# A backward pass on one core: sharing two PSUM copies between two engines, and reordering loads and small products in the weight-gradient tail

## The chip, the cores and the metric

The kernel runs on one core of one Trainium2 chip. The metric is the device time of one launch in microseconds (us), lower is better. The core has five engines that matter here, each with its own instruction queue which it works off in order: TensorE (PE in the profile; its weight loads are PEld), VectorE (DVE), ScalarE (ACT), GpSimd (POOL) and SyncE (SP). In this kernel POOL and SP mostly issue DMAs.

## The reference, cut to what matters

The reference is a training step of one transformer block: it returns the output and the gradients of all weights and of the input.

```python
h  = x + A(layernorm(x), mem0, Wq, Wk, Wv, Wo)      # attention over 64 segments of 32 tokens
h2 = h + (silu(n @ w_gate) * (n @ w_up)) @ w_down    # n = layernorm(h)

# A, for each segment s in turn:
hh = concat(mem, xs)                  # 8 memory rows + 32 tokens = 40 rows
q, k, v = hh @ Wq, hh @ Wk, hh @ Wv   # 16 heads of 256
p = softmax(mask(q k^T / 16)); o = (p v) @ Wo
mem = o[:8]                           # goes to the next segment
out = o[8:]

grads = vjp(h2)(grad_out)             # x, mem0, Wq, Wk, Wv, Wo, w_gate, w_up, w_down
```

The sizes are 2048 tokens, width 448, 16 heads of 256 (4096 columns in all), 1792 feed-forward columns, everything in bf16. The memory rows link the segments: forward they run from segment 0 to 63, backward from 63 to 0.

## The kernel before, in words

The kernel has four stages: the forward chain over the 64 segments, the feed-forward block with its backward, the backward chain over the 64 segments (`backward_chain`), and the weight gradients (`tail_phase`). A scheduler orders the instructions of each engine from priorities and data dependences; `tc.issue_after(x)` holds an instruction behind x. Once built, each engine's order is fixed.

**A backward segment.** TensorE first forms dO transposed (L1151, 128 matmuls), which is copied out of PSUM into `doT`. It then transposes dO to token-major form in two halves of eight transposes (`token_major(0)` and `(1)`, L1160); each half fills one PSUM tile `ph` of 128 x 1024 bf16 and is copied to `dO_sb` by the line that the change touches (L1161). L1169 forms dP in `pD`. VectorE turns it into dS in a chain of its own: L1176, the sum L1178, L1179 and L1181, which writes `dS_bd`. In VectorE's queue copies of head products (L75, the helper `evac`) stand between these; L76 is the same helper on ScalarE. The head products (L1128) come three times: for v they read `dO_sb` and P, for k they read Q and `dS_bd`, for q they read K and the turned dS, `dST_bd` (transposed at L1209). `rows_in` (L1200) multiplies the copied head products by the weights and sums them in `pH`. At the end L1218 and L1219 copy `pH`, L1222 sums four strips of it with `sel`, and L1226 writes the gradient of the memory rows into `do_roll`, from which the next segment's L1151 starts.

Four segments make a token tile t; r = s % 4 is the place in it, counted down. When r is 0 the tile is done, and 96 matmuls at L1264 with L1271 and L1279 behind them work on its memory rows and the layer norm. These have no place of their own: the scheduler spreads them over the next segments, L1264 over r = 3, 2 and 1, L1271 into r = 1.

**The tail.** Each group accumulates products over 16 or 20 row blocks in PSUM. `rows_by_d` (L1397) does so for Wo and w_down, `d_by_e` for the others. `d_by_e` handles width 448 as three full 128-row parts (L1375) and one 64-row part (L1380); `att` calls it for v, k, q in two halves of the heads each, passes hi = 0 to 5, each with q = 0 and q = 1; `up_grad` calls it for w_gate's and w_up's gradients, for two column parts each, after hi = 0 and hi = 2. The parameter `frees` says where the 64-row products go: if true after every four blocks, if false all at the end. It is false for the first half of each pair of calls.

In `att` the last four blocks are memory rows. They are fetched by POOL (L1340), packed by VectorE and ScalarE (L1345, L1347), transposed by TensorE in two steps through one PSUM buffer `ph` (L1354), and copied into the block's slot. `k.last_mm` is the matmul behind which these transposes are held. Two of the four fetches of a pass are issued ahead of it, two by the pass itself.

**The loads.** `_TailLoads` issues the tail's first loads on SP, in the last backward segment: `grads(0)` brings the gradient rows into `DCt` (L342 for four blocks of memory rows, then L346 and L347 in four strips), `outs` brings the stored attention outputs X_o into the slots of a ring (L356), `grads(1)` brings the last memory rows (L349). SP also issues the store of the mem0 gradient (L1232), the load of XN (L1236) and the last transpose (L1242), whose result POOL stores to DHb (L1244); L349 reads it back. The order of blocks is 16, 17, 18, 19, 15, 14, down to 0. POOL loads `grad_out` into `GO` after w_up's gradient (L1471); it is read by the last group, w_down.

Of the kernel before, what the change touches and what calls it, by code (L numbers as in the profile page):

```python
# [15 lines left out]
P = 128  # L16
# [297 lines left out]
class _TailLoads:  # L314
# [18 lines left out]
    def grads(self, part):  # L333
        k, D, S, NT, M, SEG = self.k, self.k.D, self.k.S, self.k.NT, self.k.M, self.k.SEG
        sync, DHb = k.nc.sync, k.dr["DHb"]
        dcx = DHb[0:S, 0:D].rearrange("(t r i) d -> r i t d", r=4, i=SEG)
        dcm = DHb[S:, 0:D].rearrange("(t r m) d -> r m t d", r=4, m=M)
        dc8 = DHb[0:S, 0:D].rearrange("(g s i) d -> g s i d", s=16, i=SEG)
        if part == 0:
            for g in range(k.NB - NT):  # L340
                with k.tc.issue_after(k.last_load.ins):
                    sync.dma_start(out=self.DCt[:, NT + g], in_=dc8[g, :, 0:M])  # L342
        for r in range(4):
            if part == 0:
                with k.tc.issue_after(k.last_load.ins):
                    sync.dma_start(out=self.DCt[32 * r:32 * r + 24, :NT], in_=dcx[r, M:SEG])  # L346
                    sync.dma_start(out=self.DCt[32 * r + 24:32 * r + 32, 4:NT], in_=dcm[r, :, 4:NT])  # L347
            else:
                sync.dma_start(out=self.DCt[32 * r + 24:32 * r + 32, 0:4], in_=dcm[r, :, 0:4])  # L349
# [682 lines left out]
def backward_chain(k: _K):  # L1032
    nc, tc = k.nc, k.tc
    S, D, M, H, Dh, HD = k.S, k.D, k.M, k.H, k.Dh, k.HD
    SEG, L, NSEG, NT, KC, DP, MC, DC = k.SEG, k.L, k.NSEG, k.NT, k.KC, k.DP, k.MC, k.DC
# [14 lines left out]
    dO_sb = A(52, 16, P)  # L1050
# [80 lines left out]
    for s in range(NSEG - 1, -1, -1):  # L1131
# [12 lines left out]
        with k.prio.crit():  # L1144
            pss = [k.ps1() for _ in range(4)]
            for j in range(MC):
                c = cj(j)
                b, jj = divmod(j, 8)
                for kc in range(KC):
                    with tc.issue_after(k.last_dh.ins) if s == NSEG - 1 and j == 0 and kc == 0 else nullcontext():  # L1150
                        nc.tensor.matmul(pss[b][:, jj * L:(jj + 1) * L], lhsT=WoT_sb[:, kc, c * P:(c + 1) * P],  # L1151
                                         rhs=do_roll[:, kc, sl, :], start=(kc == 0), stop=(kc == KC - 1))
# [3 lines left out]
            def token_major(hf):  # L1156
                ph = k.ps1()[:].bitcast(BF16)
                for i in range(8):
                    c0 = 2 * (8 * hf + i)
                    nc.tensor.transpose(ph[:, i * P:(i + 1) * P], doT[:, c0:c0 + 2, :].rearrange("p c n -> p (c n)"), ident[:, :])  # L1160
                nc.scalar.copy(out=dO_sb[:, 8 * hf:8 * hf + 8, :], in_=ph.rearrange("p (c n) -> p c n", n=P))  # L1161
            token_major(0)
            token_major(1)
            pD = k.ps1()
# [5 lines left out]
                                         start=(dc == 0), stop=(dc == DC - 1), skip_group_check=True)  # L1170
            if s == 0:
                k.tl.grads(0)
                k.tl.outs(0, 7, 0, 6)
            pD3 = pD[:, 0:8 * L].rearrange("p (h n) -> p h n", n=L)
            prod = k.f32("f2", 8 * L, "prod")[:].rearrange("p (h n) -> p h n", n=L)
            nc.vector.scalar_tensor_tensor(out=prod, in0=pD3, scalar=k.scale, in1=P_sb, op0=ALU.mult, op1=ALU.mult)  # L1176
# [112 lines left out]
def tail_phase(k: _K):  # L1289
# [72 lines left out]
    tl.outs(0, NB, 11, 16)  # L1362
    xo = tl.x

    def d_by_e(lhs_of, rhs_of, nblk, widths, store, at=None, frees=True):

        pa = accs(7)
        for b0 in range(0, nblk, 4):
            for fn in (at or {}).get(b0, ()):
                fn()  # L1370
            for b in range(b0, min(nblk, b0 + 4)):
                for kc in range(KC - 1):
                    for g in range(2):
                        w = widths[g]
                        k.last_mm = nc.tensor.matmul(pa[2 * kc + g][:, 0:w], lhsT=lhs_of(b)[:, kc * P:(kc + 1) * P], rhs=rhs_of(b, g),  # L1375
                                         start=(b == 0), stop=(b == nblk - 1), skip_group_check=True)
            for b in range(b0, min(nblk, b0 + 4)) if frees else range(nblk) if b0 + 4 >= nblk else ():
                for g in range(2):
                    w = widths[g]
                    k.last_mm = nc.tensor.matmul(pa[6][64 * g:64 * g + 64, 0:w], lhsT=lhs_of(b)[:, (KC - 1) * P:D], rhs=rhs_of(b, g),  # L1380
                                     start=(b == 0), stop=(b == nblk - 1), skip_group_check=True)
        for i in range(6):
            kc, g = divmod(i, 2)
            res = resbuf()
            evac(res[:, 0:widths[g]], pa[i][:, 0:widths[g]])
            store(kc, g, res[:, 0:widths[g]])
        res = resbuf()
        for g in range(2):
            evac(res[64 * g:64 * g + 64, 0:widths[g]], pa[6][64 * g:64 * g + 64, 0:widths[g]])
            store(KC - 1, g, res[64 * g:64 * g + 64, 0:widths[g]])  # L1390
# [29 lines left out]
    def att(hi, mem, after):  # L1420
        nm, oi, hf = halves[hi]
        o2 = OUT[oi].rearrange("d h e -> d (h e)")
        xt = load_x(nm, hf)
        for g in range(NG):
            xt[NT + g] = ring()
        for q in range(2):
            at = {}
            if q == 0:
                (f0, p0, t0), (f1, p1, t1), (f2, p2, t2), (f3, p3, t3) = mem
                at = {0: [p0, f2], 4: [lambda: t0(xt[NT]), p1, f3], 8: [lambda: t1(xt[NT + 1]), p2],  # L1430
                      12: [lambda: t2(xt[NT + 2]), p3], 16: [lambda: t3(xt[NT + 3])]}
            elif after is not None:
                at = {12: [after[0][0], after[1][0]]}

            def st(kc, g, r, q=q, hf=hf, o2=o2):
                e0 = (16 * g + 8 * hf + 4 * q) * P
                nc.gpsimd.dma_start(out=o2[kc * P:min(D, (kc + 1) * P), e0:e0 + 512], in_=r)  # L1437

            def rhs(b, g, q=q, xt=xt):
                return xt[b].rearrange("p (cl g n) -> p cl g n", g=2, n=P)[:, 4 * q:4 * q + 4, g, :]  # L1440
            d_by_e(lambda b: HC[:, b, :], rhs, NB, (512, 512), st, at, q == 1)

    def up_grad(nm, oi, after):
        xt = []
        for t in range(NT):
            x_t = ring()
            nc.sync.dma_start(out=x_t[:, 0:F], in_=dr[nm][t * P:(t + 1) * P, :])
            xt.append(x_t)
        for p0 in (0, 1024):
            ws = (512, min(512, F - p0 - 512))  # L1450

            def st(kc, g, r, p0=p0, oi=oi):
                f0 = p0 + 512 * g
                nc.gpsimd.dma_start(out=OUT[oi][kc * P:min(D, (kc + 1) * P), f0:f0 + r.shape[-1]], in_=r)

            def rhs(b, g, p0=p0, ws=ws, xt=xt):
                return xt[b][:, p0 + 512 * g:p0 + 512 * g + ws[g]]
            d_by_e(lambda b: HN[:, b, :], rhs, NT, ws, st, {8: [after[0][0], after[1][0]]} if p0 else None, p0 > 0)

    mems = [load_m(nm, hf) for (nm, _, hf) in halves] + [None]  # L1460
    mems[0][0][0]()
# [1 line left out]
    for hi in range(len(halves)):  # L1463
        att(hi, mems[hi], mems[hi + 1] if hi not in (0, 2) else None)
        if hi == 0:
            nc.gpsimd.dma_start(out=HN[:, 0:NT, :], in_=dr["HN"].rearrange("(t p) d -> p t d", p=P))
            up_grad("DGP", 7, mems[1])
        if hi == 2:
            up_grad("DU", 8, mems[3])
            GO = W(0, NB, D)  # L1470
            nc.gpsimd.dma_start(out=GO[:, 0:NT, :], in_=GO2.rearrange("(t p) d -> p t d", p=P))  # L1471

# [44 lines left out]
```

## Time and profile before

| | |
|---|---|
| median of 4 runs | 3098.64 us (3093.57 to 3112.2) |
| profiled execution: time, span of the core | 3099.75 us, 3097.9 us |
| TensorE busy, share of span | 2903.9 us, 94% |
| VectorE, ScalarE, GpSimd busy | 1333.8, 1114.0, 672.8 us |
| ScalarE copies at L1161 | 128 of 1015 ns mean, 123.3 us |
| backward chain, first and last L1151 | 1343.1 to 2387.3 us |
| first tail matmul | 2419.18 us |

The profile is one execution. In a timeline each row gives the start and the length in us, the engine, the line, what it writes and reads with its shape, and the number of instructions merged into the row; in brackets stands how long the engine had been idle and what ended that. Matmul ends are modelled, so the start of the next instruction says more than the end of a row. SP and POOL rows are the times of issuing a DMA, not of its landing.

### The profile page before, as it was taken

Reading aid. Unit: us, or ns where it says so; the run is one execution under the profiler, and the core shown is the slowest. Engines: PE = TensorE matmul, PEld = TensorE weight load, DVE = VectorE, ACT = ScalarE, POOL = GpSimd, SP = SyncE. Lnnn points to the kernel's source line nnn. Section 1 sums busy time; section 2 is a strip of 40 time slices with the busy share of each in tenths; the row PEclk is TensorE's granted clock in tenths of the full one; section 3 lists DMA queues with packets and bytes.
Section 4 is the critical chain, followed back from the end, with each engine's and each line's share of the span. In section 5 each row is a group of like instructions: output and inputs, shape, how many; then the busy total and the mean of one; then the engine's idle time right before and its main releaser. Section 6 shows DMA issues by size and latency. Waiting matters only on the chain.

```text
span 3097.9 us, 108337 instructions
## 1 busy us (share of the span) xinstructions
PE 2903.9 (94%) x47640; PEld 1738.6 (56%) x47650; DVE 1333.8 (43%) x3381; ACT 1114.0 (36%) x2634; POOL 672.8 (22%) x1507
## 2 busy tenths in 40 slices
PE   5999999999998999989999999999999899999999
PEld 3455555555554556666666666666666454444444
DVE  4555555555555577744444445444454001111110
ACT  2444444444444444434444344444443011111110
POOL 2222222222222222421221112212121111212111
PEclk9999999999999999999999999999999899999999
DMA  7566766766766999974554445545545998969961
GB/s 243 136 169 178 183 169 176 188 168 173 190 179 177 287 221 226 218 273 121 153 138 133 139 135 136 152 132 142 140 132 140 285 271 220 182 186 221 170 170 51
DMA packets 739468, 550.12 MB, mean 178 GB/s; under 512 B 600052, under 2 KB 635364, under 8 KB 736564
## 3 DMA queue, kind: packets, MB, share of 16 engines
q1 hardware_dynamic: 687956, 389.65, 52.3%
q0 software_dynamic: 51040, 153.54, 14.9%
q8 instruction: 374, 6.13, 0.8%
q14 instruction: 98, 0.80, 0.1%
HBM read 168.01 MB, written 234.23 MB: 130 GB/s over the span
## 4 chain that ended last, share of the span: by engine, by line
PE 65%; issue 15%; DMA 7%; DVE 6%; ACT 3%; POOL 2%; SPq 1%; POOLq 0%; ACTq 0%; DVEq 0%
PE po L1200 7%; PE psf L1151 7%; PE psf L535 6%; PE psf L652 5%; PE po L697 4%; PE psf L1128 4%; PE psf L890 4%; PE fx L1264 3%; PE fx L1014 2%; PE fx L464 2%; PE psf L1222 2%; DVE arA L75 2%; PE psf L549 2%; PE psf L1160 2%; PE psf L1397 2%
## 5 line engine op out<-in xcount | busy, mean ns | idle before, releaser
L75 DVE CAST arA<-psf 128x256 bf16<-128x256 f32 (+3 forms) x933 | 428.2, 480 | 784.6 <-PE psf L1375 233.7
L76 ACT CAST arA<-psf 128x96 bf16<-128x96 f32 (+5 forms) x915 | 353.1, 409 | 1015.4 <-PE psf L1375 254.7
L1200 PE MATMUL po<-arW,arA 128*32 128x448 bf16 x6144 | 346.2, 354 | 5.7 <-DMA arW<-Tq 3.3
L1375 PE MATMUL psf<-arW,arA 128*128 128x512 bf16 x980 | 249.9, 383 | 0.0
L1375 PEld LDWEIGHTS <-arA 128*128 128x128 bf16 x1440 | 137.0, 99 | 167.6 <-issue 18.6
L1151 PEld LDWEIGHTS <-arW 128*128 128x128 bf16 x8192 | 214.8, 96 | 25.1 <-issue 25.1
L1151 PE MATMUL psf<-arA,arW 128*128 128x40 bf16 x8192 | 218.2, 180 | 6.2 <-DVE arA L1226 5.1
L1200 PEld LDWEIGHTS <-arA 128*32 128x32 bf16 x6144 | 151.5, 96 | 116.2 <-ACT arA L76 9.5
L652 PE MATMUL psf<-arW,arA 128*64 128x512 bf16 x1536 | 216.5, 382 | 0.0
L535 PE MATMUL psf<-arW,arA 128*32 128x512 bf16 x3072 | 193.9, 385 | 12.6 <-DVE arA L738 12.6
L76 ACT CAST arB<-psf 128x64 bf16<-128x64 f32 (+3 forms) x384 | 121.9, 318 | 151.6 <-PE psf L539 106.7
L697 PE MATMUL po<-arW,arA 128*32 128x256 bf16 (+1 forms) x4096 | 141.2, 263 | 10.8 <-DVE arA L75 7.7
L890 PE MATMUL psf<-arW 128*128 128x256 bf16 (+1 forms) x1288 | 146.4, 274 | 3.0 <-DVE arA L75 1.7
L890 PEld LDWEIGHTS <-arW 128*128 128x128 bf16 (+1 forms) x1344 | 102.4, 97 | 53.3 <-issue 42.5
L1397 PE MATMUL psf<-arW 128*128 128x448 bf16 x525 | 113.0, 357 | 12.3 <-DMA arW<-X_o 12.3
L1161 ACT COPY arA<-psf 128x1024 bf16<-128x1024 bf16 x128 | 123.3, 1015 | 2.4 <-PE psf L1160 1.0
L1128 PEld LDWEIGHTS <-arW 128*128 128x128 bf16 x2048 | 86.4, 99 | 62.3 <-issue 58.1
L535 PEld LDWEIGHTS <-arA 128*32 128x32 bf16 x3072 | 70.4, 96 | 90.1 <-DVE arA L738 18.1
L76 ACT COPY arA<-psf 128x512 bf16<-128x512 bf16 (+3 forms) x142 | 84.3, 594 | 89.2 <-DVE arA L75 77.4
L464 PE MATMUL fx<-arA,arW 128*128 128x64 bf16 (+1 forms) x2048 | 84.6, 196 | 32.5 <-ACT arB L76 19.0
L697 PEld LDWEIGHTS <-arA 128*32 128x32 bf16 x4096 | 93.6, 96 | 32.9 <-DVE arA L75 11.1
L1437 POOL DMA_DIRECT2D out_dram<-arA x96 | 51.9, 547 | 275.0 <-DVE arA L75 274.6
(286 smaller groups left out, 4626.7 us busy)
## 6 DMA issues: line engine op xcount, KB each, us to landing
arW<-T SPq DMA_DIRECT2D x256, 128.0 KB
X_o<-arA SPq DMA_DIRECT2D x37, 512.0 KB
T<-arA SPq DMA_DIRECT2D x64, 256.0 KB
X_v<-arA POOLq DMA_DIRECT2D x32, 512.0 KB, 4.8
X_k<-arA POOLq DMA_DIRECT2D x32, 512.0 KB, 3.9
X_q<-arA POOLq DMA_DIRECT2D x32, 512.0 KB, 3.2
out_dram<-arA POOLq DMA_DIRECT2D x90, 128.0 KB, 5.1
VG<-arA SPq DMA_DIRECT2D x64, 160.0 KB
```

The source lines that it names most:

```text
L75: return nc.vector.tensor_copy(out=out, in_=in_)
L76: return nc.scalar.copy(out=out, in_=in_)
L464: nc.tensor.matmul(banks[w][:, i * 64:(i + 1) * 64], lhsT=lhsT, rhs=xr[lo:hi, kc, :], start=(kc == 0 and i == 0), stop=(kc == KC - 1), ski ...
L535: nc.tensor.matmul(banks[w][32 * q:32 * q + 32, :], lhsT=hT_roll[:, kc, sl, M:L], rhs=(Wq_sb, Wk_sb)[w][:, kc, col(q, b)], start=(kc == 0) ...
L652: nc.tensor.matmul(pV[b][64 * g:64 * g + 64, 0:512], lhsT=hT_flat[:, kc, sl * L:sl * L + 64], rhs=Wv_sb[:, kc, n * 512:(n + 1) * 512], sta ...
L697: nc.tensor.matmul(pO[32 * q:32 * q + 32, 0:w], lhsT=xblk[:, j, r * SEG:(r + 1) * SEG], rhs=Wo_sb[:, cj(j), 256 * dh:256 * dh + w], start= ...
L890: nc.tensor.matmul(ps[fp][:, f2 * 256:(f2 + 1) * 256], lhsT=Wt[lo:hi, kc, c * P:(c + 1) * P], rhs=xT[lo:hi, kc, :], start=(kc == 0 and f2 ...
L1128: nc.tensor.matmul(ps[b][:, i * 2 * L:(i + 1) * 2 * L], lhsT=lhs[:, at, :], rhs=rhs_bd[:, cl // 2, :, :].rearrange("p g n -> p (g n)"), st ...
L1151: nc.tensor.matmul(pss[b][:, jj * L:(jj + 1) * L], lhsT=WoT_sb[:, kc, c * P:(c + 1) * P], rhs=do_roll[:, kc, sl, :], start=(kc == 0), stop ...
L1200: nc.tensor.matmul(pH[32 * (j % 4):32 * (j % 4) + 32, 0:D], lhsT=blk[nm][:, j, r * SEG:(r + 1) * SEG], rhs=WT[:, cj(j), :], start=(nm == " ...
L1375: k.last_mm = nc.tensor.matmul(pa[2 * kc + g][:, 0:w], lhsT=lhs_of(b)[:, kc * P:(kc + 1) * P], rhs=rhs_of(b, g), start=(b == 0), stop=(b = ...
L1397: k.last_mm = nc.tensor.matmul(pa[i][:, 0:D], lhsT=lhs_of(b, i), rhs=rhs_of(b), start=(bi == 0), stop=(bi == m + 3))
```

## The change

It has four parts.

1. The two copies of a `token_major` pair are shared: the first half is copied by VectorE, the second by ScalarE. Before, ScalarE did both.
2. The loads of X_o blocks 16 to 19 (their first six column parts) are issued in `grads(0)`, between L342 and the strips of L346 and L347. Before, they came after the strips.
3. `frees` is gone: every call of `d_by_e` does its 64-row products after every four blocks. `k.last_mm` is set by these alone.
4. The load of `GO` is written after pass hi = 3 instead of after w_up's gradient. In the built program it stands behind the two M_k fetches of pass hi = 3 on POOL, where it stood ahead of them.

```diff
@@ grads(0)
                     sync.dma_start(out=self.DCt[:, NT + g], in_=dc8[g, :, 0:M])
+            self.outs(0, k.NB - NT, 0, 6)
@@ token_major
-                nc.scalar.copy(out=dO_sb[:, 8 * hf:8 * hf + 8, :], in_=ph.rearrange("p (c n) -> p c n", n=P))
+                k.evac(dO_sb[:, 8 * hf:8 * hf + 8, :], ph.rearrange("p (c n) -> p c n", n=P), "vs"[hf])
@@ last segment
-                k.tl.outs(0, 7, 0, 6)
+                k.tl.outs(4, 7, 0, 6)
@@ d_by_e
-    def d_by_e(lhs_of, rhs_of, nblk, widths, store, at=None, frees=True):
+    def d_by_e(lhs_of, rhs_of, nblk, widths, store, at=None):
...
-                        k.last_mm = nc.tensor.matmul(pa[2 * kc + g][:, 0:w], lhsT=lhs_of(b)[:, kc * P:(kc + 1) * P], rhs=rhs_of(b, g),
+                        nc.tensor.matmul(pa[2 * kc + g][:, 0:w], lhsT=lhs_of(b)[:, kc * P:(kc + 1) * P], rhs=rhs_of(b, g),
...
-            for b in range(b0, min(nblk, b0 + 4)) if frees else range(nblk) if b0 + 4 >= nblk else ():
+            for b in range(b0, min(nblk, b0 + 4)):
@@ att, up_grad
-            d_by_e(lambda b: HC[:, b, :], rhs, NB, (512, 512), st, at, q == 1)
+            d_by_e(lambda b: HC[:, b, :], rhs, NB, (512, 512), st, at)
...
-            d_by_e(lambda b: HN[:, b, :], rhs, NT, ws, st, {8: [after[0][0], after[1][0]]} if p0 else None, p0 > 0)
+            d_by_e(lambda b: HN[:, b, :], rhs, NT, ws, st, {8: [after[0][0], after[1][0]]} if p0 else None)
@@ the passes
             up_grad("DU", 8, mems[3])
+        if hi == 3:
             GO = W(0, NB, D)
             nc.gpsimd.dma_start(out=GO[:, 0:NT, :], in_=GO2.rearrange("(t p) d -> p t d", p=P))
```

## The prediction

> **What bounds the kernel now.** The page first: TensorE is busy 94% of the span, VectorE 43%, ScalarE 36%. So a copy on another engine costs nothing by itself; what counts is where TensorE stands still, and who ends the wait. Then, stage by stage, the timelines.
>
> *Backward stage* (1343 to 2407 us, 64 segments). TensorE in one segment, start and length in us:
>
> ```profile
> 2025.43 0.69 PE L1169 MATMUL psf<-arA 128*64 128x40 bf16 x32
> 2026.14 0.46 PE L1128 MATMUL psf<-arB,arA 128*128 128x80 bf16 x8
> 2026.53 0.56 PE L1264 MATMUL fx<-arW,arA 128*32 128x448 bf16 x8
> 2027.05 0.46 PE L1128 MATMUL psf<-arB,arA 128*128 128x80 bf16 x8
> 2027.44 1.70 PE L1200 MATMUL po<-arW,arA 128*32 128x448 bf16 x32
> 2028.97 0.36 PE L1264 MATMUL fx<-arW,arA 128*32 128x448 bf16 x4
> 2029.45 0.73 PE L1128 MATMUL psf<-arB,arW 128*128 128x80 bf16 x16
> ```
>
> ScalarE and VectorE in the same segment:
>
> ```profile
> 2025.07 1.93 ACT L1161 COPY arA<-psf 128x1024 bf16<-128x1024 bf16 x2
> ...
> 2026.16 0.49 DVE L1176 SCALAR_TENSOR_TENSOR prod<-psf,arB 128x320 f32<-128x320 f32 x1 [1.91 <-PE psf L1169]
> 2026.57 0.55 DVE L75 CAST arA<-psf 128x384 bf16<-128x384 f32 x1
> 2027.04 0.47 DVE L1178 TENSOR_REDUCE rsum<-prod 128x8 f32<-128x320 f32 x1
> 2027.55 0.42 DVE L75 CAST arA<-psf 128x256 bf16<-128x256 f32 x1
> ...
> 2028.48 0.83 DVE L1181 TENSOR_TENSOR arB<-prod,arB 128x640 bf16<-128x640 f32 x1
> ```
>
> The reader is to see two waits. The second eight v head products (2027.05) wait for the second L1161 copy (done 2027.00). But the k head products (2029.45) wait for L1181 (done 2029.31), the end of a VectorE chain that begins when L1169 ends (2026.12). That chain, 3.2 us, sets the segment; TensorE's work in front of the k heads is shorter. So what the copies delay is mostly given back at L1181.
>
> *Tail* (from 2407 us). TensorE and, last, the queues:
>
> ```profile
> 2419.18 2.05 PE L1397 MATMUL psf<-arW 128*128 128x448 bf16 x5 [12.04 <-DMA arW<-X_o]
> 2439.74 3.95 PE L1397 MATMUL psf<-arW 128*128 128x448 bf16 x20
> 2562.49 1.01 PE L1354 MATMUL ph<-ident,arB 128*128 128x128 bf16 x8 [6.33 <-DVE arW L75]
> 2859.93 1.01 PE L1354 MATMUL ph<-ident,arB 128*128 128x128 bf16 x8 [6.16 <-DVE arW L75]
> ...
> 2435.96 1.34 SPq L349 DMA_DIRECT2D arW<-DHb  x4
> 2844.43 1.19 POOL L1471 DMA_DIRECT2D arW<-in_grad_out_dram  x1
> 2845.61 0.78 POOL L1340 DMA_DIRECT2D arA<-M_k  x1
> 2858.84 0.43 DVE L1345 COPY arA<-arA 128x1024 bf16<-128x1024 bf16 x1 [11.37 <-DMA arA<-M_k]
> ```
>
> TensorE waits 12.04 us for the first X_o block. In pass hi=0 and hi=3 it waits 6.33 and 6.16 us at the transposes of a member block: the copy that frees `ph` stands on VectorE behind a pack (L1345) that waits for M_v or M_k. The same place costs 1.49 us in hi=1 (2676.49), 1.40 in hi=2 (2743.65) and 0.56 in hi=4 (2934.56).
>
> **What the Trainium skill says.** "TensorEngine Tiling (Array Packing)", Key Properties: a change of tiling mode drains TensorE. The trace agrees (0.23 us for a return trip, below). "TensorE: Matmul & The Clock Gate", What's actually happening: an idle window of about 3.4 us halves the clock until a busy window has passed. It agrees: after each wait of over 6 us, 512-column matmuls come 0.43 us apart instead of 0.215 for some 4.2 us. "VectorE: DVE Perf Modes", The perf-mode tier table: a copy out of PSUM has at most the double rate, fp32 none. It agrees: VectorE's copies of 1024 bf16 columns (the `ph` rows of L75) take 690 ns, those of 512 fp32 columns 687. "DMA: Bandwidth & Descriptors", Issuing engines are not separate DMA queues: all share 16 engines. It fits the 1.8 MB load of L1471 ahead of M_k: 13.2 us to the pack, against 8.6 and 9.7 in hi=1 and hi=2, where no such load stands in front.
>
> **The change part by part.** The built order of the changed program shows what moves.
>
> 1. *Copies.* 64 of 128 L1161 copies go from ScalarE (1015 ns) to VectorE (690, the row above), in front of L1176. The copy could start at 2025.07, when its transposes are done, and end at 2025.76, 0.40 before L1176 is due: nothing delayed. ScalarE's copy starts at about 2025.5 and ends at 2026.55, so the v heads end some 0.4 us earlier. The eight L1264 matmuls are then queued behind them: the same work, reordered. In the 49 segments outside the next item the k heads still wait for L1181. The only gain is inside the chain: the 256-column cast at 2027.55 starts 0.04 after TensorE's second eight ended (2027.51), while such casts otherwise start 0.08 before the end of the operation ahead (2027.51). So 0.12 us; I take 0.11: 49 x 0.11 = **-5.4 us**. Bounds 0 (another start cost) to -8.
>
> 2. *The r = 1 segments* (15). TensorE's order changes most: six L1271 matmul passes and the eight-product gap leave the way of the k heads, and VectorE now does the 256-column cast before L1181. Before: L1169 ends at 2042.16, k heads start at 2045.97, 3.81 later. After: the chain, cast included, 3.2; saves 0.6. Then eight L1271 passes at 0.115 (0.69 for six at 2045.28) and four L1200 stand before L1209, while eight L1200 leave: +0.5. At the end, L1271 and the 0.33 us wait for L1275 are gone: -0.3. Sum -0.4 each, 15 x 0.4 = **-6 us**; bounds +2 and -11.
>
> 3. *Start of the tail.* Four X_o loads are issued ahead of the eight slow DCt loads on SP (which took 2392.35 to 2407.4). So X_o blocks 16 to 19 are there when TensorE arrives. But the fifth block keeps its place behind the same bytes, and the last four blocks of the group need the rows of L349, issued 2435.96 to 2437.3, after SP waited for the DHb store. TensorE came to them at 2439.74. The 12 us wait moves there; I take **-1 us**, bounds +2 (a cold clock after the new wait) and -4.
>
> 4. *The 64-row products (L1380)* of eight passes (six first halves of att, two of up_grad) go from one block at the end into every group of four blocks. A block is 1.29 us. With 40 L1380 together, 2580.66 to 2586.49 less one block is 4.54 us; an interleaved eight, 2596.65 to 2599.03 less one block, is 1.09. Five of these are 5.45: 0.91 for four more trips, 0.23 each. Extra trips 6 x 4 + 2 x 3 = 30: **+6.8 us**. Results leave PSUM as in the second halves today, where the next pass follows without a wait (2617.84).
>
> 5. *What 4 gives back.* At the second member block two eights have been done, 2.2 us later in TensorE's order, while the M fetch lands when it did. Waits: hi=0 6.33 to 4.1; hi=1, hi=2, hi=4 (1.49, 1.40, 0.56) gone: -2.2 - 3.4 = **-5.6 us**. The clock of hi=0 still goes cold (4.1 is over 3.4); if not, another -2.
>
> 6. *The grad_out load* is now behind both M_k fetches on POOL. M_k is issued at 2844.4 and should land by 2854; TensorE needs the copy at 2856. The 6.16 us go, and with them the half-speed stretch (2562.49 to 2566.71 is 4.2 us for work of 2.1): -6.2 - 2.1 = **-8.3 us**. Behind grad_out stand the M_q fetches for hi=4, needed 55 us later; grad_out itself is read from 3050. Bounds -2.2 (M_k late anyway, only item 4's delay helps) and -8.3.
>
> Sum: -5.4 - 6 - 1 + 6.8 - 5.6 - 8.3 = -19.5. Against the profiled execution's 3099.75 us (span 3097.9) that is 3080.2; the median, 3098.64, lies 1.1 lower: **3079 us**.
>
> **Rivals.**
> *M_k is late for another reason* (the X_q transposes that start at 2826 fill the same engines). Then item 6 gives 2.2: -13.4, 3085 us. For it: DMA is 0.90 busy there. Against: 8.6 us in hi=1 at a share of 1.11.
> *The early loads pay in full.* If L349's rows come earlier, the whole 12 us can go: 11 more, 3068 us. Against: SP's order puts the OUT2 store, the transpose and the DHb store, for which L349 waits, behind the same bytes.
> *VectorE's copy is slow, and the time is longer.* Place: the queue ahead of L1176. No row of before has both engines copying 1024 columns out of PSUM at once with TensorE writing; if VectorE's copy then takes d, the chain starts d - 1.09 later in 64 segments. It decides from d = 1.40 us (64 x 0.31 = 20). At 1.5 us: +26 - 14 (items 2 to 6) = +12, 3111 us. Against: 690 ns in the `ph` rows, at most the 1015 of ScalarE.
>
> **How the numbers follow.** A measurement here tells about 0.5%, 15.5 us, from no change. Forecast 57%, M_k late 25%, full pay 12%, slow copy 6%. The range 3064 to 3098 takes in the first three with their bounds. Below 3083: three quarters of the forecast, the full pay and a fifth of M_k late: 0.60. Slower by over 15.5: most of the last, nearly 0.05. The rest 0.35.
>
> **What would show it.** Right: L1161's line gone from ScalarE for half its count, 64 VectorE copies near 0.69 us; r = 1 segments about 0.4 shorter than 16.9, others 0.1 shorter than 16.04; no wait at L1354 in hi=3, 4 us in hi=0; a wait of several us inside the first L1397 group, whose last four blocks start at about 2439 less the backward gain. Wrong: these segments unchanged, L1354 waiting over 5 us in hi=3, or L1176 starting later after L1169.

## The result

| | before | changed kernel |
|---|---|---|
| median, us (range, runs) | 3100.37 (3084.99 to 3131.32, 64) | 3084.82 (3069.95 to 3111.58, 43) |
| ratio, with 95% interval | 1 | 0.9955 [0.9943, 0.9967] |
| profiled execution: time, span, us | 3099.75, 3097.9 | 3090.31, 3088.5 |

The change saves 13.9 us by the ratio, with an interval of 10.2 to 17.7 (0.0045, 0.0033 and 0.0057 of 3100). Forecast was 19.5. The profiled execution lies 5.5 us above the median of its own kernel, so it shows less of the gain than a typical one.

### The profile after

Lines of the changed file from L343 on are one higher than before (L1160 is now L1161, L1176 is L1177, L1354 is L1355); the copies of L1161 now run at the helper lines L75 and L76.

The groups by shape show that half of the copies moved. The columns are line, engine, operation, tiles, count, then busy us and mean ns of one, then the idle time ahead.

```profile
L76 ACT COPY arA<-psf 128x1024 bf16<-128x1024 bf16 x68 | 68.8, 1012 | 44.0 <-PE psf L1161 34.5 <-PE psf L558 5.8 <-DMA Tv<-arA 3.6
L75 DVE COPY arA<-psf 128x1024 bf16<-128x1024 bf16 x72 | 49.7, 691 | 47.0 <-PE psf L1161 42.3 <-DMA Tv<-arA 2.6 <-PE psf L866 2.0
```

64 of each row are the `dO_sb` copies, 691 ns on VectorE against 1012 on ScalarE. No copy is slow: the rival that ended slower needed 1.40 us.

A backward segment (r = 2) in the timelines of TensorE, VectorE and ScalarE:

```profile
2086.93 0.69 PE L1170 MATMUL psf<-arA 128*64 128x40 bf16 x32
2087.55 1.07 PE L1129 MATMUL psf<-arB,arA 128*128 128x80 bf16 x16
...
2090.82 0.73 PE L1129 MATMUL psf<-arB,arW 128*128 128x80 bf16 x16
...
2086.52 0.69 DVE L75 COPY arA<-psf 128x1024 bf16<-128x1024 bf16 x1 [0.76 <-PE psf L1161]
2087.67 0.49 DVE L1177 SCALAR_TENSOR_TENSOR prod<-psf,arB 128x320 f32<-128x320 f32 x1 [0.45 <-PE psf L1170]
...
2089.85 0.83 DVE L1182 TENSOR_TENSOR arB<-prod,arB 128x640 bf16<-128x640 f32 x1
...
2087.09 1.01 ACT L76 COPY arA<-psf 128x1024 bf16<-128x1024 bf16 x1 [0.54 <-PE psf L1161]
```

The reader is to see that VectorE's copy ends at 2087.21 and L1177 starts only at 2087.67, when L1170 ends: the copy is out of the chain's way. The 16 v head products run in one piece; before, their second half waited for ScalarE. And the k heads (2090.82) still start just after L1182 ends (2090.68). From the start of the dP products to the k heads it is 3.89 us, against 4.02 before (2025.43 to 2029.45).

The tail, on TensorE, VectorE and the queues:

```profile
2413.78 2.05 PE L1398 MATMUL psf<-arW,arA 128*128 128x448 bf16 x5 [13.24 <-DMA arA<-X_o]
...
2552.76 1.01 PE L1355 MATMUL ph<-ident,arB 128*128 128x128 bf16 x8 [4.14 <-DVE arW L75]
...
2848.97 1.01 PE L1355 MATMUL ph<-ident,arB 128*128 128x128 bf16 x8 [3.77 <-DVE arW L75]
...
2920.25 0.61 PE L1355 MATMUL ph<-ident,arB 128*128 128x128 bf16 x8 [1.71 <-DVE arW L75]
...
2847.89 0.43 DVE L1346 COPY arA<-arA 128x1024 bf16<-128x1024 bf16 x1 [10.07 <-DMA arA<-M_k]
2848.24 0.68 DVE L75 COPY arW<-ph 128x1024 bf16<-128x1024 bf16 x1
...
2833.75 0.78 POOL L1341 DMA_DIRECT2D arA<-M_k  x1
2834.58 0.77 POOL L1341 DMA_DIRECT2D arB<-M_k  x1
2836.64 1.16 POOL L1473 DMA_DIRECT2D arW<-in_grad_out_dram  x1 [1.29 <-DMA out_dram<-arA]
```

The X_o wait is still there (13.24 us), now behind the fourth block (the row ahead of it starts at 2400.19). The wait of hi=0 fell from 6.33 to 4.14 us as predicted; those of hi=1 and hi=2 are gone. But in hi=3, where none was expected, TensorE waits 3.77 us: M_k is issued at 2833.75, ahead of grad_out, and VectorE packs it only at 2847.89. The copy that frees `ph` stands behind that pack on VectorE and starts as it ends. In hi=4 a wait of 1.71 us stands where 0.56 was to vanish.

In this execution the first half of hi=3 takes 41.93 us against 42.67 before, where the prediction had some 7.4 us less. So one profile alone says that the move of grad_out failed. The experiments ask whether it did.

### The profile page after: what moved, and what is told of

Same layout as the page of the kernel before. It is cut to its first block, busy times and chain, and to the rows that moved or that the text cites. A ratio compares the mean times of both kernels' runs of the same rounds, so it can differ in the third digit from the quotient of the medians.

```text
span 3088.5 us, 108311 instructions
## 1 busy us (share of the span) xinstructions
PE 2910.5 (94%) x47640; PEld 1740.4 (56%) x47650; DVE 1367.9 (44%) x3445; ACT 1053.0 (34%) x2570; POOL 673.2 (22%) x1507
## 4 chain that ended last, share of the span: by engine, by line
PE 71%; issue 9%; DVE 6%; DMA 6%; ACT 4%; POOL 1%; SPq 1%; ACTq 0%; POOLq 0%; DVEq 0%
PE po L1201 7%; PE psf L1152 7%; PE psf L1376 6%; PE psf L536 6%; PE psf L653 5%; PE po L698 4%; PE psf L891 3%; PE psf L1129 3%; PE fx L1265 3%; PE fx L465 2%; PE psf L1223 2%; DVE arA L75 2%; PE fx L1015 2%; PE psf L550 2%; PE psf L1161 2%
## 5 line engine op out<-in xcount | busy, mean ns | idle before, releaser
L75 DVE CAST arA<-psf 128x256 bf16<-128x256 f32 (+3 forms) x933 | 425.6, 479 | 784.2 <-PE psf L1376 275.5
L76 ACT CAST arA<-psf 128x96 bf16<-128x96 f32 (+4 forms) x915 | 353.0, 409 | 1033.3 <-PE psf L1376 261.2
L1201 PE MATMUL po<-arW,arA 128*32 128x448 bf16 x6144 | 346.7, 355 | 6.7 <-DMA arW<-Tq 2.7
L1201 PEld LDWEIGHTS <-arA 128*32 128x32 bf16 x6144 | 158.4, 96 | 124.1 <-DVE arA L75 7.7
L536 PE MATMUL psf<-arW,arA 128*32 128x512 bf16 x3072 | 193.6, 385 | 12.6 <-DVE arA L739 12.6
L76 ACT COPY arA<-psf 128x512 bf16<-128x512 bf16 (+3 forms) x206 | 149.1, 724 | 122.0 <-DVE arA L75 77.9
L76 ACT CAST arB<-psf 128x64 bf16<-128x64 f32 (+3 forms) x384 | 121.8, 318 | 156.0 <-PE psf L540 108.2
L75 DVE COPY arA<-psf 128x512 bf16<-128x512 bf16 (+2 forms) x204 | 104.2, 511 | 103.3 <-PE psf L550 55.7
L536 PEld LDWEIGHTS <-arA 128*32 128x32 bf16 x3072 | 70.5, 96 | 90.2 <-DVE arA L739 18.1
L698 PEld LDWEIGHTS <-arA 128*32 128x32 bf16 x4096 | 93.5, 96 | 32.0 <-DVE arA L75 10.9
```

The lines of the kernel that those rows point to most:

```text
L75: return nc.vector.tensor_copy(out=out, in_=in_)
L76: return nc.scalar.copy(out=out, in_=in_)
L536: nc.tensor.matmul(banks[w][32 * q:32 * q + 32, :], lhsT=hT_roll[:, kc, sl, M:L], rhs=(Wq_sb, Wk_sb)[w][:, kc, col(q, b)], start=(kc == 0) ...
L698: nc.tensor.matmul(pO[32 * q:32 * q + 32, 0:w], lhsT=xblk[:, j, r * SEG:(r + 1) * SEG], rhs=Wo_sb[:, cj(j), 256 * dh:256 * dh + w], start= ...
L1201: nc.tensor.matmul(pH[32 * (j % 4):32 * (j % 4) + 32, 0:D], lhsT=blk[nm][:, j, r * SEG:(r + 1) * SEG], rhs=WT[:, cj(j), :], start=(nm == " ...
```

## The experiments

Two labels are crossed: **a2_sixtyfour ran part 2, the loads, and a3_loads ran part 3, the 64-row products.** Each text below is what is on record under the label, and each result is read against the other label's text.

### One part at a time

**Part 1 alone, a1_copies** (the kernel before, with this edit):

```diff
-                nc.scalar.copy(out=dO_sb[:, 8 * hf:8 * hf + 8, :], in_=ph.rearrange("p (c n) -> p c n", n=P))
+                k.evac(dO_sb[:, 8 * hf:8 * hf + 8, :], ph.rearrange("p (c n) -> p c n", n=P), "vs"[hf])
```

> The kernel before with part 1 alone (first half copied by VectorE, second by ScalarE). If the VectorE chain from L1176 to L1181 sets a segment: r = 0, 2 and 3 segments shorter by 0.11 to 0.13 us and r = 1 by 0.12, as in the changed kernel, so 7 to 8 us in all (ratio 0.9975), tail unchanged. If the copies themselves set it: 0.4 us in each of 64 segments, 26 us (ratio 0.992). If something outside the segments makes up the part of the gain that the two traces do not explain: ratio near 0.9955 with segments only 0.12 shorter.

Measured: median 3089.98 us (22 runs), ratio 0.9983 [0.997, 0.9996], that is -5.3 us. Segment lengths for r = 0, 1, 2, 3 (medians): 15.87, 16.78, 15.91, 15.91 us; before 15.98, 16.91, 16.04, 16.04; the changed kernel 15.87, 16.79, 15.91, 15.91. So part 1 makes all of the change's gain in the backward stage, 0.11 to 0.13 in every segment, as the first of the three readings has it; the 0.4 us of the second are nowhere. The r = 1 segments gain no more than the others.

Its tail, whose code is that of before, is a surprise. Timelines of TensorE, VectorE and GpSimd in pass hi=3:

```profile
2860.02 1.01 PE L1354 MATMUL ph<-ident,arB 128*128 128x128 bf16 x8 [17.51 <-DVE arW L75]
...
2858.94 0.43 DVE L1345 COPY arA<-arA 128x1024 bf16<-128x1024 bf16 x1 [22.72 <-DMA arA<-M_k]
...
2833.47 1.19 POOL L1471 DMA_DIRECT2D arW<-in_grad_out_dram  x1 [0.30 <-issue]
2834.65 0.78 POOL L1340 DMA_DIRECT2D arA<-M_k  x1
```

The same M_k fetch, in the same place behind grad_out, is packed 24.3 us after its issue, against 13.2 in the profile of before. In this one place the landing of a fetch differs between two executions by 11 us, nearly as much as the whole change is worth.

**Part 2 alone, run as a2_sixtyfour:**

```diff
                     sync.dma_start(out=self.DCt[:, NT + g], in_=dc8[g, :, 0:M])
+            self.outs(0, k.NB - NT, 0, 6)
...
-                k.tl.outs(0, 7, 0, 6)
+                k.tl.outs(4, 7, 0, 6)
```

> The kernel before with part 3 alone (64-row products after every four blocks in every call). If each extra trip between the two array shapes costs 0.23 us and the waits at L1354 shrink by 2.2 us where there are as many: +6.8 for 30 trips, -2.2 in hi=0, -2.2 in hi=3, -1.5, -1.4, -0.6 and -0.8 elsewhere: -1.9 us, no measurable change (ratio 0.9994). If the M fetches land later by as much as TensorE does: +6.8 us, ratio 1.002. Each of the two up_grad first halves, which have no member block, should be 0.69 us longer in either case.

> The kernel before with part 2 alone (four X_o loads ahead of the DCt strips). If the fifth X_o block and the rows of L349 set the first group's end: the wait of 12 us moves behind the fourth block and stays 12 to 13 us, the last four blocks of the first group start within 1 us of where they did relative to the last segment, ratio 0.9998. If the early loads pay in full: 11 to 12 us, ratio 0.9963.

Measured for the loads (label a2_sixtyfour; the second text is theirs): median 3103.08 us (14 runs), ratio 1.0008 [0.9986, 1.003]; a wait of 12.98 us behind the fourth block. No gain: the wait only moves, and the 0.9963 of the full gain lies outside the interval.

**Part 3 alone, run as a3_loads:**

```diff
-            for b in range(b0, min(nblk, b0 + 4)) if frees else range(nblk) if b0 + 4 >= nblk else ():
+            for b in range(b0, min(nblk, b0 + 4)):
...
-            d_by_e(lambda b: HC[:, b, :], rhs, NB, (512, 512), st, at, q == 1)
+            d_by_e(lambda b: HC[:, b, :], rhs, NB, (512, 512), st, at)
...
```

Measured for the 64-row products (the first text is theirs): median 3096.93 us (14 runs), ratio 0.9987 [0.9966, 1.0007], which leaves out the 1.002 of "the M fetches land later". The first halves of `up_grad` have no member fetch to wait for. Their length is the time between the last PSUM copies of two passes, here those on VectorE, in the kernel before and then in a3_loads:

```profile
2618.00 0.68 DVE L75 CAST arA<-fx 64x512 bf16<-64x512 f32 x1 [0.18 <-issue]
...
2642.40 0.68 DVE L75 CAST arA<-fx 64x512 bf16<-64x512 f32 x1 [2.77 <-issue]
```

```profile
2612.33 0.68 DVE L75 CAST arA<-fx 64x512 bf16<-64x512 f32 x1 [0.18 <-issue]
...
2637.41 0.68 DVE L75 CAST arA<-fx 64x512 bf16<-64x512 f32 x1 [0.18 <-issue]
```

That is 24.40 us and 25.08: +0.68 for three more trips, 0.23 each. The waits of hi=1, hi=2 and hi=4 are gone, that of hi=0 is 4.41.

**Part 4 alone, a4_go:**

```diff
             up_grad("DU", 8, mems[3])
+        if hi == 3:
             GO = W(0, NB, D)
...
```

> The kernel before with part 4 alone (grad_out load behind the two M_k fetches of hi=3). If grad_out ahead of M_k caused the late M_k: M_k lands within 10 us of its issue, the wait of 6.16 us at L1354 in hi=3 falls below 1 and the cold clock after it goes: -8 us, ratio 0.9974. If M_k is late for another reason (the X_q transposes on the same DMA engines): it lands some 14 us after its issue, now about 1.2 us earlier, the wait is 4.5 to 6 us: -1 us or nothing.

Measured: median 3089.51 us (22 runs), ratio 0.9977 [0.9963, 0.999], -7.1 us. Timelines of GpSimd, VectorE and TensorE in hi=3:

```profile
2832.12 0.78 POOL L1340 DMA_DIRECT2D arA<-M_k  x1 [0.34 <-issue]
2833.03 0.77 POOL L1340 DMA_DIRECT2D arB<-M_k  x1
2833.79 1.16 POOL L1472 DMA_DIRECT2D arW<-in_grad_out_dram  x1
...
2837.32 0.43 DVE L1345 COPY arA<-arA 128x1024 bf16<-128x1024 bf16 x1 [2.48 <-DMA arA<-M_k]
...
2847.66 0.43 DVE L1345 COPY arB<-arB 128x1024 bf16<-128x1024 bf16 x1 [6.66 <-DMA arB<-M_k]
...
2848.74 0.61 PE L1354 MATMUL ph<-ident,arA 128*128 128x128 bf16 x8 [1.46 <-DVE arW L75]
```

Here M_k is packed 5.2 us after its issue, and the second fetch 14.6 us after its own; so a wait of 1.46 us is left at a later block, where the text expected less than 1. The move of grad_out does work when it is taken alone, and the four parts together (-0.0017 + 0.0008 - 0.0013 - 0.0023 = -0.0045) add up to the ratio of the whole, each with an interval of 0.0013 to 0.0022 either way.

### How close is VectorE's copy to the chain?

Both runs start from the changed kernel. c1_swap gives the first half to ScalarE and the second to VectorE, so VectorE's copy begins as late as it can; c2_both_vector gives VectorE both.

```diff
@@ the changed kernel to c1_swap
-                k.evac(dO_sb[:, 8 * hf:8 * hf + 8, :], ph.rearrange("p (c n) -> p c n", n=P), "vs"[hf])
+                k.evac(dO_sb[:, 8 * hf:8 * hf + 8, :], ph.rearrange("p (c n) -> p c n", n=P), "sv"[hf])
@@ the changed kernel to c2_both_vector
-                k.evac(dO_sb[:, 8 * hf:8 * hf + 8, :], ph.rearrange("p (c n) -> p c n", n=P), "vs"[hf])
+                k.evac(dO_sb[:, 8 * hf:8 * hf + 8, :], ph.rearrange("p (c n) -> p c n", n=P), "v")
```

> The changed kernel with the engines of the two copies exchanged: ScalarE copies the first half, VectorE the second. If the VectorE chain sets a segment: VectorE's copy starts half a microsecond later and ends about when L1177 is due, which then starts 0.1 to 0.15 us later after L1170; segments of r = 3 and 2 take 16.0 us instead of 15.91, 5 to 8 us slower than the changed kernel (ratio 0.9975). If sharing the copies is what counts, whichever engine takes which: 15.91 us, ratio 0.9955.

> The changed kernel with both copies on VectorE. If the VectorE chain sets a segment: two copies of 0.69 us end some 0.25 us after L1170, L1177 starts 0.2 to 0.3 us later, segments of r = 3 and 2 take 16.1 to 16.2 us, 12 to 18 us slower than the changed kernel (ratio 1.000). If relief of ScalarE is what counts: 15.91 or less, ratio 0.9955 or below.

Measured: c1_swap 3083.31 us (17 runs), ratio 0.9938 [0.9918, 0.9958]; c2_both_vector 3086.6 (8 runs), 0.9943 [0.9913, 0.9973]. Segments: 15.87, 16.57, 15.91, 15.92 and 15.95, 16.56, 15.96, 15.96. Timelines of VectorE and TensorE, c1_swap first:

```profile
2081.42 0.69 DVE L75 COPY arA<-psf 128x1024 bf16<-128x1024 bf16 x1 [1.28 <-PE psf L1161]
2082.05 0.49 DVE L1177 SCALAR_TENSOR_TENSOR prod<-psf,arB 128x320 f32<-128x320 f32 x1
...
2081.31 0.69 PE L1170 MATMUL psf<-arA 128*64 128x40 bf16 x32
```

```profile
2082.12 1.29 DVE L75 COPY arA<-psf 128x1024 bf16<-128x1024 bf16 x2 [0.76 <-PE psf L1161]
2083.32 0.48 DVE L1177 SCALAR_TENSOR_TENSOR prod<-psf,arB 128x320 f32<-128x320 f32 x1
...
2082.53 0.69 PE L1170 MATMUL psf<-arA 128*64 128x40 bf16 x32
```

From the start of L1170 to L1177 it is 0.74 us in the changed kernel, 0.74 in c1_swap and 0.79 in c2_both_vector. So even a second-half copy is just in time. So c1_swap came out as its second text has it, at 15.91. Only two copies on VectorE delay the chain, by 0.05 us, and the segments of r = 0, 2, 3 lengthen by 0.05 to 0.08. Both delays expected were too large, but the little that c2_both_vector shows fits the first text: what L1177 loses, the segment loses. And the gain needs no second engine: with both copies on VectorE the segments still beat those of before, 15.96 against 16.04.

The 0.22 us that the r = 1 segments gain in both runs was not expected at all. TensorE and, last, VectorE in such a segment of the changed kernel:

```profile
2038.33 0.73 PE L1170 MATMUL psf<-arA 128*64 128x40 bf16 x32
2038.99 0.39 PE L1129 MATMUL psf<-arB,arA 128*128 128x80 bf16 x6
2039.31 0.37 PE L1265 MATMUL fx<-arW,arA 128*32 128x448 bf16 x3
2039.62 0.39 PE L1129 MATMUL psf<-arB,arA 128*128 128x80 bf16 x6
2039.93 0.56 PE L1265 MATMUL fx<-arW,arA 128*32 128x448 bf16 x8
...
2040.71 0.30 PE L1129 MATMUL psf<-arB,arA 128*128 128x80 bf16 x4
2040.95 1.69 PE L1201 MATMUL po<-arW,arA 128*32 128x448 bf16 x29
2042.57 0.75 PE L1129 MATMUL psf<-arB,arW 128*128 128x80 bf16 x16
...
2041.45 0.82 DVE L1182 TENSOR_TENSOR arB<-prod,arB 128x640 bf16<-128x640 f32 x1
```

and in c1_swap, TensorE:

```profile
2097.22 0.69 PE L1170 MATMUL psf<-arA 128*64 128x40 bf16 x32
2097.93 0.60 PE L1129 MATMUL psf<-arB,arA 128*128 128x80 bf16 x12
2098.47 0.75 PE L1265 MATMUL fx<-arW,arA 128*32 128x448 bf16 x11
...
2099.34 0.32 PE L1129 MATMUL psf<-arB,arA 128*128 128x80 bf16 x4
2099.58 1.69 PE L1201 MATMUL po<-arW,arA 128*32 128x448 bf16 x29
2101.20 0.75 PE L1129 MATMUL psf<-arB,arW 128*128 128x80 bf16 x16
```

In the changed kernel L1182 ends at 2042.27, but TensorE is at its 29 L1201 products until about 2042.5: the chain no longer sets this segment, TensorE's own work does. The same products stand ahead of the k heads in c1_swap, in four blocks instead of six: the twelve v heads run together and the eleven L1265 behind them. L1170 to k heads takes 3.98 us there and 4.24 here. The 0.26 between them is the size of one return trip between full-array products and 32-column products, where the 64-row products gave 0.23. "TensorEngine Tiling (Array Packing)", Key Properties, in the Trainium skill says that a change of mode drains TensorE, and gives no price; this fits, but no run changed the number of trips alone in this place.

### Are the waits at the member blocks the fetches' landing?

Eight executions have the fetches where the kernel before has them. Times are from the timelines of GpSimd, VectorE and TensorE in hi=3. M_k lands, by the profile, 0.1 us before its pack in all eight. "DMA rate" is what the core's 16 DMA engines moved between its issue and its landing. The last column is the time between the starts of the last PSUM copies of two passes. Without a wait it is 34.27 us with the 64-row products at the end (d1_late_loads below) and 35.18 with them interleaved (b2_early_pack).

| kernel | grad_out | 64-row products | M_k issue to pack | DMA rate | wait | first half of hi=3 |
|---|---|---|---|---|---|---|
| before | ahead | at the end | 13.2 us | 300 GB/s | 6.16 us | 42.67 us |
| a1_copies | ahead | at the end | 24.3 | 168 | 17.51 | 53.54 |
| a2_sixtyfour (loads) | ahead | at the end | 17.7 | 222 | 10.97 | 47.87 |
| a3_loads (64-row) | ahead | interleaved | 14.0 | 267 | 5.12 | 42.06 |
| changed kernel | behind | interleaved | 14.1 | 191 | 3.77 | 41.93 |
| a4_go | behind | at the end | 5.2 | 289 | 1.46 | 35.82 |
| c1_swap | behind | interleaved | 7.1 | 308 | none | 35.19 |
| c2_both_vector | behind | interleaved | 12.6 | 152 | 2.96 | 39.90 |

With grad_out ahead, the half exceeds its wait-free length by 12.0 us on average (6.9 to 19.3); behind, by 3.3 (0 to 6.8). Part 4 is worth some 8.8 us here, though the executions overlap and the changed kernel's own profile is among the worst of its kind. Part of the 8.8 is the interleaving, which three of the four below have and one of the four above.

The rate tells apart what part 4 does and what it doesn't. Time times rate is the amount moved by the landing: 3.7 to 4.1 MB in each of the four with grad_out ahead, 1.5 to 2.7 with it behind. The means differ by 1.85 MB, the size of grad_out. So part 4 takes these bytes out of M_k's way, but the scatter among the four with grad_out ahead is in the rate: 168 to 300 GB/s, while the profile's busy share of the DMA engines hardly differs (1.07 to 1.16). The packet records show where the rate goes. A packet of 4096 or 4480 bytes, the sizes of these loads, takes 0.2 us (median) in all eight. But between issue and landing 30 to 42 of them take over 1 us, up to 4, in the four executions of 152 to 222 GB/s (a1_copies, a2_sixtyfour, the changed kernel, c2_both_vector), seven in a3_loads and none in the other three. What holds these packets up is not shown.

If landing is the cause, an earlier fetch should end all of it. **b2_early_pack** (on the changed kernel), **b3_early_deferred** (the same, but with the 64-row products at the end of first halves as before) and **b5_early_alone** (on the kernel before, none of the four parts) move the first pack and the third fetch of a pass into the pass ahead:

```diff
-                at = {0: [p0, f2], 4: [lambda: t0(xt[NT]), p1, f3], 8: [lambda: t1(xt[NT + 1]), p2],
+                at = {4: [lambda: t0(xt[NT]), p1, f3], 8: [lambda: t1(xt[NT + 1]), p2],
...
-                at = {12: [after[0][0], after[1][0]]}
+                at = {0: [after[0][0], after[1][0]], 16: [after[0][1], after[2][0]]}
@@ up_grad, before
-            d_by_e(lambda b: HN[:, b, :], rhs, NT, ws, st, {8: [after[0][0], after[1][0]]} if p0 else None, p0 > 0)
+            d_by_e(lambda b: HN[:, b, :], rhs, NT, ws, st, {0: [after[0][0], after[1][0]], 12: [after[0][1], after[2][0]]} if p0 else None, p0 > 0)
```

The third fetch goes into the buffer that the first pack empties, so the two move together. For hi=0, which has no pass ahead of it in `att`, the first two fetches are written ahead of the load of Wo, and the first pack with the third fetch behind the load of HC.

> The changed kernel, with the first pack and the third fetch of each attention pass's member rows moved ahead: the first two fetches are issued at the start of the pass before it instead of near its end, the pack and the third fetch in that pass's last group (for hi=0 after the HC load). If the waits at L1355 come from M fetches that land anywhere from 5 to 25 us after their issue while VectorE's queue waits in a pack: no wait over 1 us at L1355 in any pass, all six first halves near 34.9 us or their own work, 10 to 15 us faster than the changed kernel, ratio to before 0.991 to 0.992. If TensorE waits there for its own turn (one ph buffer, two copies): the waits stay, ratio 0.9955.

> As b2_early_pack, but with the 64-row products at the end of the first halves again, as in the kernel before. If a trip between the two array shapes costs 0.23 us and nothing is left for it to cover: 6.8 us faster than b2_early_pack, each attention first half 0.9 us and each up_grad first half 0.69 us shorter, ratio to before 0.989. If the later turns of the interleaved order still hide a wait: equal to b2_early_pack or slower.

> The kernel before with one edit: the first pack and the third member fetch of each pass are moved into the pass ahead of it; none of the four parts of the change. Theory (the waits at the transposes of the member blocks come from the fetches' landing, and all of them go when the fetches start a half pass earlier): before's own waits 6.3 + 1.5 + 1.4 + 6.2 + 0.6 = 16 us go, with the cold stretches behind the two long ones (2 x 2.1): 20 us, on average more, since single fetches land at 15 to 25 us: ratio 0.990 to 0.993, no wait over 1 us at L1354. Then the copies (-5.4) and the grad_out load (nothing, its wait being gone) make the rest of b3_early_deferred, so b3 is 5 to 8 us below this run. Rival (the gain of b3 needs the grad_out load out of the way): this run keeps a wait of over 3 us in hi=3 and its ratio is 0.993 or above.

| | median, us (runs) | ratio to before | longest wait at a member block |
|---|---|---|---|
| b2_early_pack | 3073.69 (6) | 0.9894 [0.986, 0.9928] | none |
| b3_early_deferred | 3064.54 (6) | 0.9868 [0.9835, 0.9901] | 0.61 us, hi=0 |
| b5_early_alone | 3073.9 (6) | 0.9933 [0.9908, 0.9958] | 0.63 us, hi=0 |

All three agree: with earlier fetches no wait over 0.63 us is left at a member block. The ratio of b5_early_alone lies just inside what its text gave to the rival (0.993 or above), but the wait of over 3 us in hi=3, which belongs to the rival, is not there. That is no full test of the rival, for in b5_early_alone the earlier issue also takes the third M_k fetch out from behind grad_out (issued at 2805.79 and 2827.15 us). The fourth stands behind it, is packed 11.8 us after its issue, and TensorE doesn't wait for it. The kernel before gains 20.8 us (13.0 to 28.5) from this edit alone, against 13.9 (10.2 to 17.7) from the four parts. b3_early_deferred is 9.2 us below b2_early_pack. Their stages show why: every first half of `att` from hi=1 on is 0.91 us shorter and every one of `up_grad` 0.68; with hi=0 at the same rate that is 6.8. (In b3_early_deferred hi=0 is only 0.21 shorter, since the wait of 0.61 us stands there; in d1_late_loads below, without that wait, it is 0.91.) So once the waits are gone, part 3 is a loss of its full price.

### The best version, and the early loads once more

**b4_early_swapped** is b3_early_deferred with the engines of c1_swap. **d1_late_loads** is the same without part 2; **d2_early_loads** is b4_early_swapped again, on the chip of d1_late_loads.

```diff
@@ b3_early_deferred to b4_early_swapped and d2_early_loads
-                k.evac(dO_sb[:, 8 * hf:8 * hf + 8, :], ph.rearrange("p (c n) -> p c n", n=P), "vs"[hf])
+                k.evac(dO_sb[:, 8 * hf:8 * hf + 8, :], ph.rearrange("p (c n) -> p c n", n=P), "sv"[hf])
@@ d2_early_loads to d1_late_loads
-            self.outs(0, k.NB - NT, 0, 6)
...
-                k.tl.outs(4, 7, 0, 6)
+                k.tl.outs(0, 7, 0, 6)
```

> The kernel of b3_early_deferred (early fetch and pack, 64-row products at the end of first halves as before, the other three parts of the change), with ScalarE copying the first half of each token-major pair and VectorE the second. Theory (the VectorE chain has room, and the swapped order shortens only the r = 1 segments, 16.79 to 16.57 in c1_swap): 15 x 0.22 = 3.3 us less than b3_early_deferred, ratio to before 0.985 to 0.987, segments 15.87/16.57/15.91/15.91. Rival (the 16.57 is tied to where the scheduler put L1272 in that one build and is given back elsewhere): ratio 0.987 or above, within 1 us of b3_early_deferred.

> The kernel of b4_early_swapped without part 2: the X_o loads of blocks 16 to 19 stand behind the strips again, as before. Theory (part 2 moves the wait for the X_o blocks by four blocks and then costs a little: over the seven profiles with it the time from the last segment to the end of group 6 is 159.7 us on average, over the five without it 157.6): last segment to group 6 about 2 us shorter than in d2_early_loads, a wait of about 12 us ahead of the first L1397 group and none inside the second, time 2 us below d2_early_loads, ratio 0.984 to 0.990. Rival (part 2 is worth its predicted 1 us, the averages being noise between runs): 1 us above d2_early_loads.

> b4_early_swapped once more, on the same chip as d1_late_loads, to compare with: parts 1 (swapped engines), 2 and 4, early fetch and pack. Ratio 0.986 to 0.991; a wait of 13 to 15 us inside the first L1398 group, and 0.8 to 1.8 us in the second.

Measured: b4_early_swapped 3067.79 us (6 runs), ratio 0.9907 [0.9884, 0.9929]; d2_early_loads, the same kernel, 3063.92 (6), 0.9884 [0.9855, 0.9914]. The r = 1 segments take 16.57 us in both, as the theory said, but the 3 us that follow from it are not seen in the ratios, which lie where the rival put them. b4_early_swapped waits 1.72 us in hi=0, the one wait over 1 us at a member block among the kernels with early fetches; d2_early_loads, the same kernel, 0.26. Against b5_early_alone on its own chip b4_early_swapped is 6.1 us faster. d1_late_loads has 3062.59 (6), 0.9886 [0.9856, 0.9916]. GpSimd, VectorE and TensorE of d1_late_loads in hi=3:

```profile
2795.08 0.78 POOL L1340 DMA_DIRECT2D arA<-M_k  x1 [0.54 <-ACT arA L1347]
...
2818.64 0.42 DVE L1345 COPY arA<-arA 128x1024 bf16<-128x1024 bf16 x1
...
2829.69 0.61 PE L1354 MATMUL ph<-ident,arA 128*128 128x128 bf16 x8
```

The third M_k fetch is issued 23.6 us ahead of its pack, the pack waits for nothing, and neither do the transposes.

From the last backward segment to the end of group 6, d1_late_loads takes 159.4 us and d2_early_loads 160.8. Over all profiles the mean is 159.8 for the eight with part 2 and 157.9 for the six without. With part 2 the X_o waits are longer on average, 13.6 us against 11.9 in the first group and 1.1 against 0.4 in the second; but d1_late_loads itself waits 13.42 and 0.72, more than its text expected. Part 2 thus seems to cost about 2 us instead of saving one. This is not shown: the single kernels overlap, the totals of d1 and d2 don't differ, and why the wait gets longer was not found.

The versions with early fetches, shared copies and the 64-row products at the end are the fastest here: 3062.6 to 3067.8 us, 26 to 37 below the kernel before on the same chip. Which of b3, b4 and d1 is best stays open.

## Why the prediction was right, and where its sizes were off

| step | forecast, us | what the runs show, us | from |
|---|---|---|---|
| 1 copies, 49 segments | -5.4 | -6.0 | segments 0.11 (r = 0) or 0.13 (r = 2, 3) shorter |
| 2 r = 1 segments | -6 | -1.8 | 15 x 0.12 |
| 3 start of the tail | -1 | about +2 | mean of 8 profiles against 6, overlapping |
| 4 64-row products | +6.8 | +6.8 | 6 x 0.91 + 2 x 0.68 |
| 5 hi=0, 1, 2, 4 | -5.6 | -5.5 | mean of four profiles each way |
| 6 grad_out | -8.3 | -7.1 (-11.5 to -3.1) | ratio of a4_go |
| sum | -19.5 | -11.6 | |
| ratio of the whole | | -13.9 (-17.7 to -10.2) | |

The right-hand sum lies inside the interval of the whole, so nothing large need be left over.

**Step 1** held with its mechanism: VectorE's cast no longer waits for the second v head products, and the chain, as long as before otherwise, ends earlier. The removed copies themselves bought nothing, as the prediction said.

**Step 2** is the term that was mis-sized most, by 4.2 us. The prediction let the k heads start when the chain ends, 3.2 us after L1169 ends. The chain was as forecast (2039.06 to 2042.27), but the k heads start at 2042.57, 3.51 us after: TensorE was busy with the products that the changed order leaves there. The next term, +0.5, measured +0.38 (k to q heads, 2.95 to 3.33), and the last, -0.3, measured -0.20 (q heads to the next L1151, 5.19 to 4.99). So -0.12 in place of -0.4. The sum priced the instructions that moved and not how often TensorE changes between tile shapes. That this made the difference is likely but not isolated: c1_swap has one such return trip fewer and gains 0.22.

**Step 3** had the wait's new place right and its sign, it seems, wrong. That is another 3 us, less certain than step 2's.

**Step 4** was right to 0.1 us, in every kernel that has it.

**Step 5** was right as a sum but not pass by pass. Over their wait-free lengths, the first halves of hi=0, 1, 2 and 4 lose 15.5 us in the four executions of the table above with the products at the end, and 10.0 in the four with them interleaved. In the changed kernel's profile hi=1 and hi=2 lose nothing, but hi=4 loses 1.8; in c1_swap it is hi=1 that loses 7.3. Single executions of one order lose between 6.0 and 20.5 in all, so that 5.6 came out as 5.5 is luck. The list also left out the wait of 0.80 us in hi=5, which goes as well.

**Step 6** was argued from one execution and read a chance as a rule. The prediction took 13.2 us in hi=3 against 8.6 and 9.7 elsewhere for the price of the load ahead. But the fetches of one and the same code are packed 13.2, 14.0, 17.7 and 24.3 us after issue with grad_out ahead, and 5.2, 7.1, 12.6 and 14.1 with it behind. The load does matter, by the 1.8 MB that it puts ahead. That the size of the step came out near its forecast is in part luck: on average the half lost more before (12.0 us, where the one profile has 8.4) and kept a loss of 3.3 after, where the forecast had none. "M_k should land by 2854", that is within 10 us, did not hold: in two of four executions it takes longer. So the rival "M_k is late for another reason" fits the changed kernel's own profile, and the forecast fits the difference of the means. That the median fell within 1 us of that rival's 3085 is step 2's and step 3's doing.

The two other rivals are out: VectorE's copy takes 0.69 us, in c1_swap too, where ScalarE's copy (2080.96 to 2081.97) overlaps it by 0.55 us, and the early loads left the whole wait standing.

## What to carry to other kernels

Where a wait in a profile ends at a DMA, look at several executions before you price it: here one fetch in unchanged code came 13 or 24 us after its issue, and a profile of the changed kernel alone would have called a useful part useless. Ask also how much was moved until the landing, and at what rate: here the reordering changed the amount, and the scatter was in the rate. If a landing time scatters like that, don't try to shorten it by a few us; issue the fetch a whole stage earlier, and take its consumer out of the queue in front of a copy that others wait for. And before deleting a cheap-looking way of grouping small products, count the changes of tile shape: once the waits that hid them were gone, 30 return trips cost about 7 us.

## What was not expected of the hardware

- The third member fetch of hi=3 (512 KB, in pieces of 1024 bytes by the profile) takes 13.2 to 24.3 us from issue to its pack with the same loads ahead of it, and 5.2 to 14.1 without grad_out. By the table, the core's DMA engines move 152 to 191 GB/s meanwhile in the three slowest of the eight and 289 to 308 in the three fastest, and what differs is a few dozen packets that take 1 to 4 us instead of 0.2.
- Two VectorE copies of 128 x 1024 bf16 in a row take 1.29 us together, 0.09 less than twice one.
- The clock fell to half after waits shorter than the 3.4 us that the prediction went by. After a wait of 2.82 us (c2_both_vector, hi=4, the lines below) the eight transposes still take 0.61 us, but the five 512-column products soon behind them take 2.34 us, where five take 1.24 at full speed. After 2.96 us (hi=3) the transposes themselves take 1.01. Over all profiles, each of the 18 waits of 2.82 us or more at these transposes is followed by such a stretch, and none of the seven from 1.40 to 2.40. So 4.1 us in place of 6.3 didn't save the cold stretch.

```profile
2915.60 0.61 PE L1355 MATMUL ph<-ident,arB 128*128 128x128 bf16 x8 [2.82 <-DVE arW L75]
...
2916.79 2.34 PE L1376 MATMUL psf<-arW,arA 128*128 128x512 bf16 x5
...
2920.75 1.24 PE L1376 MATMUL psf<-arW,arA 128*128 128x512 bf16 x5
```
